# Sliding-window decode attention with a gated mixer: head outputs collected by one product a unit, one product for shared maxima, another order at the end, and 30 instead of 28 weight blocks summed in shares

## The chip, the core and the metric

The kernel runs on one core of one Trainium2 chip. A core has five engines that run side by side, each in its own program order: PE (TensorE, matrix products; its weight loads are listed as PEld), DVE (VectorE), ACT (ScalarE), POOL (GpSimd) and SP (SyncE, which here only issues transfers). They meet through semaphores. Sixteen DMA engines move data between HBM, where inputs and outputs lie, and SBUF; PE writes its sums to PSUM banks, from which DVE and ACT read. The metric is the device time in microseconds (us) of one execution; lower is better.

## The reference

One token is decoded for each of two batches. With `x` the input of width 512, everything in float32:

```python
xn = _layernorm(x)
# attention: 32 query heads on 8 key/value heads, the last W = 4096 of 32768 cached positions
q = (xn @ wq)                                      # wq 512 x 4096
scores = einsum("bhqd,bhkd->bhqk", q, k) * 128**-0.5
s = einsum("bhqk,bhkd->bhqd", softmax(scores), v)  # head width 128
s = s.reshape(2, 1, 4096) @ wo                     # wo 4096 x 512
# gated mixer: one more small feed-forward of xn
z = gelu(xn @ w_in); z1, z2 = halves(z); z2 = _layernorm(z2)
g = silu((z1 * (w_sp * z2 + b_sp)) @ w_out)
return x + s * g
```

Of the caches only the window is read: 2 batches x 8 heads x 4096 x 128 x 4 bytes, 33.5 MB of keys and as many of values. With `wq` and `wo` (8.4 MB each), `w_in` and `w_out` the page counts 89.40 MB read from HBM.

## The kernel before

**Tiles and ring.** Work is cut into 8 *units*; a unit is one batch and two key/value heads, so its keys fill one tile of 128 partitions x 8192 numbers (4 MB) and its values another. All large loads go through one ring of four such slots, in the order `win, wout, wq0, wq1, k0, k1, v0, k2, v1, ... k7, v6, v7, wo0, wo1, wo2`, all issued by SP in that order. A load can be issued only when the last reader of the tile four places before it in the ring is done; what stands behind it on SP waits with it. So `wo2`, the last 2 MB of the output weights, takes the slot of `v6`, the values of unit 6, and `wo1` that of `k7`. `wo` is cut into 32 blocks of 256 KB: `wo0` brings 16 of them in two transfers of 8, `wo1` brings 8 in one, and `wo2` brings blocks 24 to 31 in transfers of 4, 2, 1 and 1 blocks (`pieces`). A block is a tile of 128 x 512.

**One unit.** `turn` has DVE transpose a quarter of the keys in 32 x 32 squares (`kt`, four a unit). `shares` multiplies it on PE by the query heads, in four groups of 32 columns of the array (`sh`), and ACT copies the result to SBUF (`shs`). `add_shares` adds the shares of the four groups in another product (`s`). `share_max` finds the maximum of each head's scores: DVE reduces (`m`), spreads the maxima with a mask (`mg`), PE multiplies by `same_r` so that all partitions of a head see all its maxima (`mo`), DVE reduces again (`mx`) and makes the bias (`nb`). `probs` is the exponential on ACT (`p`, sums `l`), `weights` and `weigh` add the sums over the partitions of a head and invert them (`ls`, `wd`), `probs_t` transposes `p` (`pT`). `values` is the product with the values: 16 products of 512 columns, in four column groups (`acc`). `scale_out` copies `acc` to SBUF on ACT, scaled (`o`, four calls). `collect` puts the unit's eight head outputs into rows of a PSUM bank that the units of a batch share (`col`), and `gather` reduces that bank, after a batch's last unit, to `oT`, the outputs in the layout that the final product needs. PE sums float32 in two records per product, so the profile counts each product twice.

**Order.** Every helper records its instruction to be kept in program order, so each engine does its work in the order of the code, and the profile shows nearly all of it at one line, L37. The loop over units runs one unit ahead: while unit n's keys are turned and multiplied, unit n-1 (`prev`) gets its maxima, exponentials and values. After the loop stands what is left of unit 7.

**The end.** `part` sums blocks 0 to `EARLY`-1 of the final product in four column groups, block n in group n mod 4, each with all 512 output columns. When all are summed, ACT copies the bank (`parts`), and `spread_quarters` adds the four groups while it cuts the 512 columns in quarters (`so`, 4 products of 128 columns). The blocks from `EARLY` on are added straight to `so`, four products of 128 columns for each block. DVE multiplies by the gate and adds `x` (`res`), and SP and ACT write the two rows of the output.

Of the kernel before, what the change touches and what calls it, by code (L numbers as in the profile page):

```python
# [12 lines left out]
AX = mybir.AxisListType  # L13

P = 128
HQ, DH = 32, 128
G = 4
# [4 lines left out]
def ap(t, offset, dims):  # L22

    return bass.AP(tensor=t.tensor, offset=t.offset + offset, ap=[list(t.ap[0])] + [list(d) for d in dims])
# [18 lines left out]
def kernel(  # L43
# [13 lines left out]
    nc = tc.nc  # L57
    pe, dve, act, sp = (InOrder(tc, e) for e in (nc.tensor, nc.vector, nc.scalar, nc.sync))
    B, _, D = x.shape
# [9 lines left out]
    NU = B * HKV // 2  # L69
    J = 2 * W // P  # L70
    JC = 512 // 32
    NCH = J // JC
# [8 lines left out]
    def slot(name):  # L81
        return ring.tile([P, SLOT], F32, tag="slot", name=name)

    def const(name, *shape):
        return cst.tile([P, *shape], F32, tag=name, name=name)

    def bank(name, tag):
        return ps.tile([P, 512], F32, tag=tag, name=name, bufs=BANKS[tag])
# [12 lines left out]
    for a in range(2):  # L101
        t = slot(f"wq{a}")
# [29 lines left out]
    nc.gpsimd.memset(x4, 0.0)  # L132
    add_dq = const("add_dq", NCH - 1 + P)
    nc.gpsimd.memset(add_dq, 0.0)
    sel = const("sel", 35)
    nc.gpsimd.memset(sel, 0.0)
    oT = const("oT", 32, 32)
    nc.gpsimd.memset(oT, 0.0)

    rowm = const("rowm", 32)  # L140
# [32 lines left out]
    rowr = const("rowr", 8)  # L173
    dve.tensor_reduce(rowr, rowm.rearrange("p (r m) -> p r m", m=NCH), axis=AX.X, op=ALU.add)
    same_r = const("same_r", G, 8, NCH)
    dve.tensor_copy(same_r, ap(rowr, 0, [[0, G], [1, 8], [0, NCH]]))
    same_r = same_r.rearrange("p g r m -> p (g r m)")
    diag = const("diag", NCH)
    dve.tensor_reduce(diag, rowm.rearrange("p (r m) -> p m r", m=NCH), axis=AX.X, op=ALU.add)
    dve.tensor_copy(sel[:, 3:35:4], rowr)  # L180
    for a in range(2):
        dve.tensor_copy(
            ap(add_dq, NCH - 1 + 16 * a, [[32, G], [4, REP]]),
# [14 lines left out]
    for k in range(KT):  # L198
        for g in range(G):
            pe.matmul(  # L200
                pz[32 * g : 32 * g + 32, :], xnT[:, k, :], ap(win[:, k, :], g * FQ, [[FH, 2], [1, FQ]]),
                start=(k == 0), stop=(k == KT - 1),
# [43 lines left out]
    def spread_quarters(dst, shares, start=True, stop=True):  # L246
        for g in range(G):
            pe.matmul(
                dst[32 * g : 32 * g + 32, :], rowm, shares[:, g * DC : (g + 1) * DC], start=start, stop=stop,
            )  # L250
# [18 lines left out]
    for k in range(KT):  # L269
        for r in range(2):  # L270
            for g in range(G):
# [3 lines left out]
                    start=(k == 0), stop=(k == KT - 1),  # L275
# [24 lines left out]
    def turn(u, m):  # L300

        u.kt[m] = sb.tile([P, JC, DH], F32, tag="kt", name=f"kt{u.n}_{m}", bufs=3)
        dve.transpose(
            u.kt[m].rearrange("p j d -> p (j d)"), u.k[:, JC * m : JC * m + JC, :].rearrange("p j d -> p (j d)")
        )

    def shares(u, m):

        u.sh = bank(f"sh{u.n}_{m}", "sh")
        for dq in range(4):  # L310
            pe.matmul(
                u.sh[32 * dq : 32 * dq + 32, :], q_of(u, dq), u.kt[m][:, :, 32 * dq : 32 * dq + 32],
                start=True, stop=True,
            )
        u.shs[m] = sb.tile([P, 512], F32, tag="shs", name=f"shs{u.n}_{m}")
        act.activation(u.shs[m], u.sh, AF.Copy)

    def add_shares(u, m):

        if m == 0:  # L320
            u.s = bank(f"s{u.n}", "s")
        pe.matmul(u.s, add_dq[:, NCH - 1 - m : NCH - 1 - m + P], u.shs[m], start=(m == 0), stop=(m == NCH - 1))

    def share_max(u):
        m2 = sb.tile([P, 2], F32, tag="m2", name=f"m2_{u.n}")
        dve.tensor_reduce(m2, ap(u.s, 0, [[1, 2], [2, 256]]), axis=AX.X, op=ALU.max)
        mg = sb.tile([P, 2, G * NCH], F32, tag="mg", name=f"mg{u.n}")
        dve.tensor_mul(mg, ap(m2, 0, [[1, 2], [0, G * NCH]]), spot.rearrange("p a g m -> p a (g m)"))
        u.mo = bank(f"mo{u.n}", "mo")
        for a in range(2):  # L330
            pe.matmul(u.mo[:, : G * NCH], same_r, mg[:, a], start=(a == 0), stop=(a == 1))
        mx = sb.tile([P, 1], F32, tag="mx", name=f"mx{u.n}")
        dve.reduce_max(mx, u.mo[:, : G * NCH], axis=AX.X)
        u.nb = sb.tile([P, 2], F32, tag="nb", name=f"nb{u.n}")
        dve.scalar_tensor_tensor(u.nb, ap(mx, 0, [[0, 2]]), -SCALE, negm, op0=ALU.mult, op1=ALU.add)

    def probs(u):

        u.p = sb.tile([P, 512], F32, tag="p", name=f"p{u.n}")
        u.l = sb.tile([P, 2], F32, tag="l", name=f"l{u.n}")  # L340
        for a in range(2):
            act.activation(
                ap(u.p, a, [[2, 256]]), ap(u.s, a, [[2, 256]]), AF.Exp,
                bias=u.nb[:, a : a + 1], scale=SCALE, accum_out=u.l[:, a : a + 1],
            )

    def probs_t(u):
        u.pT = sb.tile([P, JC, 32], F32, tag="pT", name=f"pT{u.n}")
        dve.transpose(u.pT.rearrange("p j r -> p (j r)"), u.p)

    def weights(u):
        pe.matmul(u.mo[:, 32:34], same_r, u.l, start=True, stop=True)

    def weigh(u):
        l = sb.tile([P, 1], F32, tag="ls", name=f"ls{u.n}")
        dve.reduce_sum(l, u.mo[:, 32:34], axis=AX.X)
        dve.reciprocal(l, l)
        u.wd = sb.tile([P, NCH], F32, tag="wd", name=f"wd{u.n}")
        dve.tensor_scalar_mul(u.wd, diag, l)

    def values(u):
        u.acc = bank(f"acc{u.n}", "acc")
        for j in range(JC):
            c = j % G
            pe.matmul(
                u.acc[32 * c : 32 * c + 32, :], u.pT[:, j, :], u.v[:, j : J : JC, :],
                start=(j < G), stop=(j >= JC - G),
            )

    def scale_out(u):  # L370
        u.o = sb.tile([P, 4, DH], F32, tag="o", name=f"o{u.n}")
        for jj in range(4):
            act.activation(
                u.o[:, jj, :], u.acc[:, jj * DH : (jj + 1) * DH], AF.Copy, scale=u.wd[:, jj : jj + 1]
            )

    col = {}

    def collect(u):
        if u.w == 0:  # L380
            col[u.b] = bank(f"col{u.b}", "col")[:, : 4 * 32].rearrange("p (j d) -> p j d", j=4)
        for e in range(4):
            pe.matmul(
                col[u.b][32 * u.w : 32 * u.w + 32], sel[:, 3 - e : 35 - e], u.o[:, :, 32 * e : 32 * e + 32],
                start=(e == 0), stop=(e == 3),
            )

    def gather(u):
        if u.w == NU // B - 1:
            dve.reduce_sum(oT[:, :, 16 * u.b], col[u.b].rearrange("p j d -> p d j"), axis=AX.X)  # L390

    units = []
    for n in range(NU):
        u = Unit()
# [13 lines left out]
    j = 0  # L408
    for i, piece in enumerate(pieces):
        t = slot(f"wo{i}").rearrange("p (j d) -> p j d", d=D)  # L410
        at = 0
        for n in piece:
            sp.dma_start(t[:, at : at + n, :], wo_v[:, j : j + n, :])
            blocks += [(t, at + a) for a in range(n)]
            at, j = at + n, j + n
# [2 lines left out]
                    sp.dma_start(x4[16 * b : P : 32, :], by_group(x, b, 0, DC))  # L418

    prev = old = None  # L420
    for u in units:
        turn(u, 0)
        shares(u, 0)
        if old is not None:
            gather(old)
        if prev is not None:
            share_max(prev)
            probs(prev)
            weights(prev)
        turn(u, 1)  # L430
        shares(u, 1)
        add_shares(u, 0)
        if prev is not None:
            probs_t(prev)
            weigh(prev)
            values(prev)
        for m in range(2, NCH):
            turn(u, m)
            shares(u, m)
            add_shares(u, m - 1)  # L440
        if prev is not None:
            scale_out(prev)
        add_shares(u, NCH - 1)
        if prev is not None:
            collect(prev)
        old, prev = prev, u
    share_max(prev)
    probs(prev)
    weights(prev)
    probs_t(prev)  # L450
    weigh(prev)
    values(prev)
    scale_out(prev)
    collect(prev)
    gather(prev)


    EARLY = 28
    part = bank("part", "sh")
    for n in range(EARLY):  # L460
        t, a = blocks[n]
        g = n % G
        pe.matmul(part[32 * g : 32 * g + 32, :], oT[:, n, :], t[:, a, :], start=(n < G), stop=(n >= EARLY - G))
    parts = sb.tile([P, D], F32, tag="shs", name="parts")
    act.activation(parts, part, AF.Copy)
    so = bank("so", "mo")[:, :DC]
    spread_quarters(so, parts, stop=False)
    for n in range(EARLY, 32):
        t, a = blocks[n]
# [37 lines left out]
```

## Time and profile before

| what | us |
|---|---|
| median of 3 runs (lowest to highest) | 218.58 (218.48 to 218.61) |
| the profiled execution's own time | 218.74 |
| its span, first to last instruction | 216.9 |
| PE busy in the span | 155.2 |
| DVE busy | 105.8 |
| ACT busy | 43.9 |
| DVE idle before the key transposes | 45.9, of it 38.6 until keys landed |

The profile is of one execution. A row of a group of instructions gives the line, the engine, the operation, the tiles (out<-in), the shapes and the count, then the busy time and the mean of one in ns, then the engine's idle time just before them and what ended it. "DMA x" as a releaser is the landing of a transfer. In views by time, columns are the start and the length in us. Engines that are idle off the path to the end cost nothing, so the busy shares alone don't tell the bound.

### The profile page before, as it was taken

How to read it: one execution, taken by the hardware profiler on the slowest of the kernel's cores; microseconds unless marked ns; L12 is line 12 of the kernel's file. 1: busy time of each engine (PE TensorE's matmuls, PEld its weight loads, DVE VectorE, ACT ScalarE, POOL GpSimd, SP SyncE). 2: the span in 40 equal slices, each digit the busy share in tenths (PEclk: the TensorE clock that was granted, in tenths of full speed). 3: DMA queues.
4: the chain of work that ended last, by engine and by line, in shares of the span. 5: the costliest groups of instructions: out<-in, count | busy, mean ns of one | idle time of the engine just before them, and what ended most of it. 6: DMA issues, size and time to landing. Idle time of an engine off the chain costs nothing.

```text
span 216.9 us, 2315 instructions
## 1 busy us (share of the span) xinstructions
PE 155.2 (72%) x914; PEld 48.6 (22%) x914; DVE 105.8 (49%) x165; ACT 43.9 (20%) x109; POOL 2.5 (1%) x13
## 2 busy tenths in 40 slices
PE   0173189409959948975997698499759958979672
PEld 0121022101212222222223122222321231232221
DVE  3405402659687089247806932890595189121001
ACT  5003310002221421032114203211330421140200
POOL 4000000000000000000000000000000000000000
PEclk9997559955988995998599799859966996996999
DMA  7999999999999999999999999999999999999980
GB/s 249 428 435 465 405 461 408 447 423 435 423 429 435 420 447 411 453 411 447 424 438 429 435 426 423 435 435 432 423 441 417 453 411 435 432 411 415 425 334 3
DMA packets 3937, 89.54 MB, mean 413 GB/s; under 512 B 454, under 2 KB 470, under 8 KB 856
## 3 DMA queue, kind: packets, MB, share of 16 engines
q1 hardware_dynamic: 3912, 89.40, 96.4%
q8 instruction: 7, 0.11, 0.2%
q14 instruction: 2, 0.02, 0.0%
q10 hardware_dynamic: 16, 0.01, 0.0%
HBM read 89.40 MB, written 0.00 MB: 412 GB/s over the span
## 4 chain that ended last, share of the span: by engine, by line
DMA 66%; DVE 18%; PE 14%; issue 1%; ACT 0%; DVEq 0%; ACTq 0%
DMA k<-in_A_k_cache_dram 50%; DVE kt L37 16%; DMA wo<-in_A_wo_dram 11%; DMA win<-in_B_w_in_dram 5%; PE sh L37 5%; PE s L37 3%; PE z L37 2%; PE acc L37 2%; PE mo L37 1%; DVE pT L37 1%; PE so L37 1%; PE part L37 1%; DVE mx L37 0%; DVE ls L37 0%; DVE wd L37 0%
## 5 line engine op out<-in xcount | busy, mean ns | idle before, releaser
L37 DVE STREAM_TRANSPOSE kt<-k 128x2048 f32<-128x2048 f32 x32 | 72.7, 2295 | 45.9 <-DMA k<-in_A_k_cache_dram 38.6
L37 PE MATMUL sh<-kt,qbd 128*32 128x512 f32 x256 | 41.3, 721 | 19.1 <-DVE kt L37 19.1
L37 ACT ACTIVATE shs<-sh 128x512 f32<-128x512 f32 x32 | 19.1, 597 | 123.4 <-PE sh L37 123.4
L37 PE MATMUL s<-shs,add_dq 128*128 128x512 f32 x64 | 40.6, 741 | 0.0
L37 PE MATMUL acc<-v,pT 128*32 128x512 f32 x256 | 34.1, 680 | 0.4 <-DVE ls L37 0.4
L37 PEld LDWEIGHTS s<-shs,add_dq 128*128 128x128 f32 x64 | 11.3, 219 | 30.8 <-issue 26.4
L37 PEld LDWEIGHTS acc<-v,pT 128*32 128x32 f32 x256 | 8.3, 125 | 29.2 <-issue 18.4
L37 PEld LDWEIGHTS sh<-kt,qbd 128*32 128x32 f32 x256 | 6.3, 115 | 35.0 <-issue 19.5
L37 PE MATMUL mo<-l,same_r 128*128 128x2 f32 x16 | 3.5, 287 | 12.2 <-ACT p L37 12.2
L37 ACT ACTIVATE o<-acc,wd 128x128 f32<-128x128 f32 x32 | 9.1, 373 | 6.2 <-PE acc L37 6.2
L37 PE MATMUL col<-o,sel 128*32 128x128 f32 x64 | 8.5, 275 | 1.3 <-ACT o L37 1.3
L37 DVE TENSOR_REDUCE m<-s 128x2 f32<-128x512 f32 x8 | 5.3, 664 | 7.6 <-PE s L37 7.6
L37 PE MATMUL z<-win,xnT 128*32 128x448 f32 x32 | 5.0, 789 | 5.4 <-DMA win<-in_B_w_in_dram 5.4
L37 ACT ACTIVATE p<-s,nb 128x256 f32<-128x256 f32 x16 | 7.6, 485 | 4.3 <-DVE nb L37 4.3
L37 PEld LDWEIGHTS col<-o,sel 128*32 128x32 f32 x64 | 6.3, 109 | 7.6 <-ACT o L37 6.9
L37 PE MATMUL q_ps<-wq,xnT 128*32 128x512 f32 x64 | 7.7, 633 | 0.0
L37 PE MATMUL part<-wo,oT 128*32 128x512 f32 x56 | 6.4, 595 | 1.3 <-DMA wo<-in_A_wo_dram 0.8
L37 PE MATMUL y<-wout,hT 128*32 128x512 f32 x14 | 3.6, 1058 | 3.8 <-issue 3.8
L37 DVE STREAM_TRANSPOSE pT<-p 128x512 f32<-128x512 f32 x8 | 5.4, 674 | 1.1 <-ACT p L37 1.1
L37 PEld LDWEIGHTS mo<-l,same_r 128*128 128x128 f32 x16 | 2.8, 219 | 13.0 <-ACT p L37 13.0
L37 PEld LDWEIGHTS mo<-mg,same_r 128*128 128x128 f32 x32 | 4.2, 190 | 6.2 <-DVE mg L37 6.2
L37 ACT ACT_TABLE_LOAD x4 | 5.1, 1283 | 2.0 <-issue 1.9
(100 smaller groups left out, 54.8 us busy)
## 6 DMA issues: line engine op xcount, KB each, us to landing
k<-in_A_k_cache_dram SPq DMA_DIRECT2D x8, 4096.0 KB, 26.5
v<-in_A_v_cache_dram SPq DMA_DIRECT2D x8, 4096.0 KB, 33.5
wq<-in_A_wq_dram SPq DMA_DIRECT2D x2, 4096.0 KB, 29.2
wo<-in_A_wo_dram SPq DMA_DIRECT2D x3, 2048.0 KB, 28.2
win<-in_B_w_in_dram SPq DMA_DIRECT2D x1, 3584.0 KB
wout<-in_B_w_out_dram SPq DMA_DIRECT2D x1, 1792.0 KB, 15.3
wo<-in_A_wo_dram SPq DMA_DIRECT2D x1, 1024.0 KB, 22.9
wo<-in_A_wo_dram SPq DMA_DIRECT2D x1, 512.0 KB, 23.8
```

What stands on the lines that cost most here:

```text
L37: return self.tc.keep_in_program_order(call(*args, **kwargs))
```

## The change

Four things change.

1. `collect` becomes one product a unit: the whole `o` (128 x 512) against 32 columns of a mask, into the rows of the unit's batch in one `col` bank. `gather` then does more, once a batch: DVE reduces the bank to `heads` (32 x 128), four small products with the new mask `place` spread the heads over 128 partitions in a PSUM bank of the `acc` kind, and DVE copies the result to `oT`. `place` is cleared by POOL and filled by DVE at the start, `sel` grows from 35 to 56 columns.
2. `share_max` adds the two halves of `mg` on DVE and makes one product with `same_r` of it, where there were two.
3. In the last pass of the loop (unit 7), the values of unit 6, their scaling and their collecting are left out. They stand after the loop, the values in two halves: one ahead of unit 7's maxima, one behind its exponentials. `scale_out` and `collect` of unit 6 stand among unit 7's steps.
4. `EARLY` goes from 28 to 30. Blocks 28 and 29 (the transfer of two blocks) are now summed into `part`, ahead of the copy `parts`; only blocks 30 and 31 come behind the spread.

```diff
-        for a in range(2):
-            pe.matmul(u.mo[:, : G * NCH], same_r, mg[:, a], start=(a == 0), stop=(a == 1))
+        dve.tensor_add(mg[:, 0], mg[:, 0], mg[:, 1])
+        pe.matmul(u.mo[:, : G * NCH], same_r, mg[:, 0], start=True, stop=True)
...
-    def values(u):
-        u.acc = bank(f"acc{u.n}", "acc")
-        for j in range(JC):
+    def values(u, part=0, parts=1):
+        if part == 0:
+            u.acc = bank(f"acc{u.n}", "acc")
+        n = JC // parts
+        for j in range(n * part, n * part + n):
...
     def collect(u):
...
+        r = slice(32 * u.b, 32 * u.b + 32)
+        pe.matmul(
+            col[0][r, :], sel[:, 24 - 8 * u.w : 56 - 8 * u.w], u.o.rearrange("p j d -> p (j d)"),
+            start=(u.w == 0), stop=(u.w == NU // B - 1),
+        )
+
+    def gather(u):
+
+        if u.w < NU // B - 1:
+            return
+        r = slice(32 * u.b, 32 * u.b + 32)
+        dve.reduce_sum(heads[r, :], col[0][r, :].rearrange("p (j d) -> p d j", j=NCH), axis=AX.X)
+        t = bank(f"oT{u.b}", "acc")[:, :32]
         for e in range(4):
             pe.matmul(
-                col[u.b][32 * u.w : 32 * u.w + 32], sel[:, 3 - e : 35 - e], u.o[:, :, 32 * e : 32 * e + 32],
-                start=(e == 0), stop=(e == 3),
-            )
-
-    def gather(u):
-        if u.w == NU // B - 1:
-            dve.reduce_sum(oT[:, :, 16 * u.b], col[u.b].rearrange("p j d -> p d j"), axis=AX.X)
+                t, place[r, 3 - e : 3 - e + P], heads[r, 32 * e : 32 * e + 32], start=(e == 0), stop=(e == 3)
+            )
+        dve.tensor_copy(oT[:, :, 16 * u.b], t)
...
-            values(prev)
+            if u is not last:
+                values(prev)
...
-    share_max(prev)
-    probs(prev)
...
+    values(old, 0, 2)
+    share_max(last)
+    probs(last)
+    values(old, 1, 2)
+    weights(last)
+    probs_t(last)
+    weigh(last)
+    scale_out(old)
+    values(last)
+    collect(old)
+    scale_out(last)
+    collect(last)
+    gather(last)
+
+
+    EARLY = 30
```

On PE the end of the program, from the last key products of unit 7 on, reads before (a row is one run of like products; "32x512 x16" is sixteen products with 32 rows and 512 columns of output):

```order
L37 MATMUL acc_948<-v_305,pT_941 32x512 x16
L37 MATMUL sh_2_967<-kt_2_965,qbd 32x512 x4
L37 MATMUL s_939<-shs_1_937,add_dq 128x512
L37 MATMUL sh_3_977<-kt_3_975,qbd 32x512 x4
L37 MATMUL s_939<-shs_2_972,add_dq 128x512
L37 MATMUL s_939<-shs_3_982,add_dq 128x512
L37 MATMUL col_810<-o_985,sel 32x128 x4
L37 MATMUL mo_999<-mg_997,same_r 128x16 x2
L37 MATMUL mo_999<-l_1007,same_r 128x2
L37 MATMUL acc_1018<-v_307,pT_1011 32x512 x16
```

and after:

```order
L37 MATMUL sh_2_941<-kt_2_939,qbd 32x512 x4
L37 MATMUL s_930<-shs_1_928,add_dq 128x512
L37 MATMUL sh_3_951<-kt_3_949,qbd 32x512 x4
L37 MATMUL s_930<-shs_2_946,add_dq 128x512
L37 MATMUL s_930<-shs_3_956,add_dq 128x512
L37 MATMUL acc_960<-v_309,pT_932 32x512 x8
L37 MATMUL mo_973<-mg_971,same_r 128x16
L37 MATMUL acc_960<-v_309,pT_932 32x512 x8
L37 MATMUL mo_973<-l_981,same_r 128x2
L37 MATMUL acc_1005<-v_311,pT_993 32x512 x16
```

The values of unit 6 (the first `acc` row of each list) moved from ahead of unit 7's third key product to behind its last score product, in two halves around the product of the maxima.

The rows that follow these on PE, up to the end of the program, read before:

```order
L37 MATMUL col_810<-o_1035,sel 32x128 x4
L37 MATMUL part<-wo_309,oT 32x512 x16
L37 MATMUL part<-wo_314,oT 32x512 x8
L37 MATMUL part<-wo_316,oT 32x512 x4
L37 MATMUL so<-parts,rowm 32x128 x4
L37 MATMUL so<-wo_316,oT 32x128 x16
```

and after:

```order
L37 MATMUL col<-o_1000,sel 32x512
L37 MATMUL col<-o_1023,sel 32x512
L37 MATMUL oT_1030<-heads,place 128x32 x4
L37 MATMUL part<-wo_313,oT 32x512 x16
L37 MATMUL part<-wo_318,oT 32x512 x8
L37 MATMUL part<-wo_320,oT 32x512 x6
L37 MATMUL so<-parts,rowm 32x128 x4
L37 MATMUL so<-wo_320,oT 32x128 x8
```

Two blocks of `wo2` moved from behind the spread (`so<-parts`) to ahead of it, and `oT` is now made by way of four small products.

On DVE the steps of unit 7 from its maxima on read after (before, the rows with `mg` as only input, with `heads` and with COPY are not there, and a reduction `oT<-col` stands in place of the last two):

```order
L37 TENSOR_REDUCE m_7_969<-s_930 128x2
L37 TENSOR_TENSOR mg_971<-m_7_969,spot 128x32
L37 TENSOR_TENSOR mg_971<-mg_971 128x16
L37 TENSOR_REDUCE mx_976<-mo_973 128x1
L37 TENSOR_SCALAR nb_978<-mx_976,negm 128x2
L37 STREAM_TRANSPOSE pT_993<-p_980 128x512
L37 TENSOR_REDUCE ls_995<-mo_973 128x1
L37 RECIPROCAL ls_995<-ls_995 128x1
L37 TENSOR_SCALAR wd_998<-diag,ls_995 128x4
L37 TENSOR_REDUCE heads<-col 32x128
L37 COPY oT<-oT_1030 128x32
```

One addition per unit and one copy per batch came to DVE. On SP the transfers stand in the same order before and after.

More of the change, by code (lines that the diff above doesn't have):

```diff
@@ L134 @@
     nc.gpsimd.memset(add_dq, 0.0)
-    sel = const("sel", 35)
+    sel = const("sel", 56)
     nc.gpsimd.memset(sel, 0.0)
+    place = const("place", 3 + P)
+    nc.gpsimd.memset(place, 0.0)
+    heads = const("heads", DH)
     oT = const("oT", 32, 32)
@@ L179 @@
     dve.tensor_reduce(diag, rowm.rearrange("p (r m) -> p m r", m=NCH), axis=AX.X, op=ALU.add)
-    dve.tensor_copy(sel[:, 3:35:4], rowr)
+    dve.tensor_copy(sel[:, 24:32], rowr)
+    dve.tensor_copy(place[:, 3 : 3 + P : 4], rowm)
     for a in range(2):
@@ L379, in collect @@
     def collect(u):
-        if u.w == 0:
-            col[u.b] = bank(f"col{u.b}", "col")[:, : 4 * 32].rearrange("p (j d) -> p j d", j=4)
+        if u.n == 0:
+            col[0] = bank("col", "col")
+        r = slice(32 * u.b, 32 * u.b + 32)
[9 more added lines that the diff above has]
+        t = bank(f"oT{u.b}", "acc")[:, :32]
         for e in range(4):
             pe.matmul(
-                col[u.b][32 * u.w : 32 * u.w + 32], sel[:, 3 - e : 35 - e], u.o[:, :, 32 * e : 32 * e + 32],
-                start=(e == 0), stop=(e == 3),
-            )
-    def gather(u):
-        if u.w == NU // B - 1:
-            dve.reduce_sum(oT[:, :, 16 * u.b], col[u.b].rearrange("p j d -> p d j"), axis=AX.X)
+                t, place[r, 3 - e : 3 - e + P], heads[r, 32 * e : 32 * e + 32], start=(e == 0), stop=(e == 3)
+            )
+        dve.tensor_copy(oT[:, :, 16 * u.b], t)
     units = []
@@ L420 @@
     prev = old = None
+    last = units[-1]
     for u in units:
@@ L440 @@
             add_shares(u, m - 1)
-        if prev is not None:
+        if u is not last and prev is not None:
             scale_out(prev)
         add_shares(u, NCH - 1)
-        if prev is not None:
+        if u is not last and prev is not None:
             collect(prev)
         old, prev = prev, u
-    share_max(prev)
-    probs(prev)
[L449 to L458, printed above, removed]
+    values(old, 0, 2)
[12 more added lines that the diff above has]
+    EARLY = 30
     part = bank("part", "sh")
```

## The prediction

> **What bounds the kernel now.** I read the page's head first, then the chain that ended last, then the end of the timeline, and last the transfer queue against that timeline.
>
> ```profile
> span 216.9 us, 2315 instructions
> ...
> DMA  7999999999999999999999999999999999999980
> ...
> DMA 66%; DVE 18%; PE 14%; issue 1%; ACT 0%; DVEq 0%; ACTq 0%
> ...
> L37 DVE STREAM_TRANSPOSE kt<-k 128x2048 f32<-128x2048 f32 x32 | 72.7, 2295 | 45.9 <-DMA k<-in_A_k_cache_dram 38.6
> ```
>
> The DMA engines are at 9 tenths or more in 38 of the 40 slices. PE, at 72% of the span, is far from that, and DVE stands 38.6 us waiting for keys. The transfers set the pace; the engines have room in every unit.
>
> The chain's last pieces (start, length, what):
>
> ```profile
> 183.50 3.62 PE acc L37 x32
> ...
> 187.13 22.94 DMA wo<-in_A_wo_dram
> 210.07 0.04 issue
> 210.12 1.11 PE part L37 x8
> ...
> 211.31 0.61 ACT parts L37
> ...
> 211.96 1.34 PE so L37 x40
> ...
> 213.32 0.30 DVE res L37
> ```
>
> The 1 MB transfer with blocks 24 to 27 is issued when the values of unit 6 are done (187.13) and lands at 210.07. What comes after it is bare: four blocks, the copy, the spread and four more blocks, 213.30 at the end. Between issue and landing lie 22.94 us for one MB, so it only stands in a queue. Are the other two MB of the tail on time? Their issues by SP, and the mean times to landing:
>
> ```profile
> 187.51 0.43 SPq L37 DMA_DIRECT2D wo<-in_A_wo_dram  x1
> 197.12 0.33 SPq L37 DMA_DIRECT2D wo<-in_A_wo_dram  x1
> wo<-in_A_wo_dram SPq DMA_DIRECT2D x1, 512.0 KB, 23.8
> DMA to landing us min/median/max: 15.5/22.9/28.2
> ```
>
> Blocks 28 and 29 (512 KB) land at 187.51 + 23.8 = 211.3; block 31, issued last and with the shortest time to landing, at 197.12 + 15.5 = 212.6. In the kernel before both are there when PE reaches them: blocks 28 and 29 are needed behind the spread, after 211.96, and the 40 products from 211.96 on run without a stop (1.34 us for 40, each 0.27 and four side by side).
>
> Was PE itself late for 210.07? These rows say no:
>
> ```profile
> 203.54 0.29 DVE L37 TENSOR_REDUCE oT<-col 128x32 f32<-128x128 f32 x1 [7.24 <-PE col L37]
> 203.94 5.36 PE L37 MATMUL part<-wo,oT 128*32 128x512 f32 x48 [0.43 <-issue]
> 210.12 1.07 PE L37 MATMUL part<-wo,oT 128*32 128x512 f32 x8 [0.82 <-DMA wo<-in_A_wo_dram]
> ```
>
> `oT` is ready at 203.83, 24 blocks are done at 209.30, and PE idles 0.82 us until the landing. So an earlier `oT` is worth nothing here, unless the landings also come earlier.
>
> **Blocks 28 and 29 summed in shares: the term that counts.** Before, the copy waits for the landing of 210.07; after, for that of 211.31, 1.24 us later. From landing to the start of the copy it took 210.07 to 211.31 = 1.24 us with four blocks in four column groups. With two blocks in two groups I take the same 1.24: each block still needs its two passes one after the other. The nearest rows, one group alone and four side by side:
>
> ```profile
> 187.86 1.13 PE L37 MATMUL s<-shs,add_dq 128*128 128x512 f32 x2
> L37 PE MATMUL part<-wo,oT x56: 589/592/617, 203.9 to 210.6; 128*32 128x512 f32 x56
> ```
>
> One group took 1.13, four took 1.07. The bounds of the pair are thus 0.06 more, and, if all four records ran at once, one record's 0.59 in place of 1.07, 0.48 less; I take the four-group row, being of the same tiles. The copy then starts at 211.31 + 1.24 = 212.55, and PE takes up the spread 0.65 later (211.96 - 211.31), at 213.20. What is left is 24 records instead of 40: (1.34 - 0.27) / 39 = 0.027 a step, so 23 x 0.027 + 0.27 = 0.90. PE ends at 214.10 where it ended at 213.30: +0.80. Block 31 has landed at 212.6 by then. Everything behind it (`res`, the output) moves along. Bounds of this term: +0.32 to +0.86.
>
> **The new order of the last units: nothing.** It moves the values of unit 6 (3.62 us on PE) behind the last score product of unit 7, and with them the release of `v6`'s slot, for which `wo2`'s first transfer waits, with three more of `wo2` queued behind it on SP. The rows for when that is:
>
> ```profile
> 182.82 2.27 DVE L37 STREAM_TRANSPOSE kt<-k 128x2048 f32<-128x2048 f32 x1
> 188.92 1.07 PE L37 MATMUL sh<-kt,qbd 128*32 128x512 f32 x8
> 191.93 0.69 DVE L37 TENSOR_REDUCE m<-s 128x2 f32<-128x512 f32 x1 [6.84 <-PE s L37]
> 192.91 0.62 PE L37 MATMUL mo<-mg,same_r 128*128 128x16 f32 x4
> 195.85 5.34 PE L37 MATMUL acc<-v,pT 128*32 128x512 f32 x32 [0.36 <-DVE ls L37]
> 201.25 1.14 ACT L37 ACTIVATE o<-acc,wd 128x128 f32<-128x128 f32 x4 [6.20 <-PE acc L37]
> 202.44 1.06 PE L37 MATMUL col<-o,sel 128*32 128x128 f32 x8 [1.26 <-ACT o L37]
> ...
> 187.00:204.00 17.00, 13.36 (x84) 4.87 (x80) 2.66 (x9) 4.38 (x14) 0.00 (x0) 0.90 0.99 420
> ```
>
> The last keys are turned at 185.09. PE is then free for them at about 185.3, and the scores are complete 191.93 - 188.92 = 3.0 later, at 188.3. The values of unit 6 follow, 3.6 us plus the small product for the maxima, done at about 192.3. So `wo2` is issued 5.2 us later than now. In front of it in the queue stand 22.94 x 420 GB/s = 9.6 MB at 187.13, so 17.7 us remain at 192.3: hidden. If that cover were gone, each us of delay would be a us of the total. The two single blocks are not concerned: the last is issued at 197.12 by another wait.
>
> `oT` comes earlier: the maxima's product at about 190.2 (behind the first half of unit 6's values), then 195.85 - 192.91 = 2.9 to unit 7's values at 193.1, 3.6 of values (5.34 at the slower clock of that row), 1.2 for the scaling, about 1.1 for a product of 512 columns in two passes, 0.7 for the reduction of 512 numbers (as `m`), the four placing products and 0.2 for the copy. The trace has no such product. In eight records, they cost no less than the four `mo` records, 0.62; from above, two `mo` rows and their waits in full, some 8 x 0.46 = 3.7 by the means of weight load (190 ns) and product (268 ns) below. Near the `mo` row I take 0.9: `oT` at about 200.8, with the upper price 203.6, with the slower clock on top of it 205.3. 24 blocks took 5.36 with a stop, so 28 take at most 5.36 x 28 / 24 = 6.3; they must be done at 211.3, and `oT` may come as late as 205.0. Cost nothing, gain nothing.
>
> **One product for shared maxima, one product a unit for collecting.**
>
> ```profile
> L37 PE MATMUL mo<-mg,same_r 128*128 128x16 f32 x32 | 5.0, 268 | 0.0
> L37 PEld LDWEIGHTS mo<-mg,same_r 128*128 128x128 f32 x32 | 4.2, 190 | 6.2 <-DVE mg L37 6.2
> ...
> L37 DVE TENSOR_TENSOR mg<-m,spot 128x32 f32<-128x32 f32 x8 | 1.5, 192 | 0.3
> ...
> L134 POOL MEMSET add_dq<- 128x131 f32 x1 | 0.2, 207 | 0.0
> ```
>
> Per unit DVE gains an addition of at most 0.19 us (the row of `mg`, on twice the numbers) and PE loses two records of `mo`; collecting goes from 1.06 us to the 1.1 of a 512-column product in two passes. Once, in unit 5, DVE stands about 1.5 us longer in `gather`, waiting for PE in front of the next maxima. All of it lies under the 38.6 us of waiting for keys, or, for unit 7, under the slack just shown. Without that cover 8 x 0.19 + 1.5 = 3 us would show. POOL's new clear is of the size of `add_dq`'s, 0.2 us, and its results are first read at the end of the first unit and of the first batch.
>
> **The sum.** The transfers end where they did, the tail is 0.80 longer: 218.74 + 0.80 = 219.5 for the profiled execution, which lies 0.16 above the median; against the median, 218.58 + 0.80 = 219.4.
>
> **Rivals.** *PE at half clock in the tail.* The trace shows the clock fall after a stretch in which PE mostly idled:
>
> ```profile
> 193.50:197.00 3.50, 1.56 (x15) 0.71 (x18) 1.49 (x6) 1.02 (x4) 0.00 (x0) 0.99 1.01 431
> 197.00:200.40 3.40, 3.40 (x20) 0.87 (x16) 0.00 (x0) 0.00 (x0) 0.00 (x0) 0.51 1.00 425
> 206.94 0.16 PEld L37 LDWEIGHTS part<-wo,oT 128*32 128x32 f32 x4 [0.27 <-DMA wo<-in_A_wo_dram]
> ```
>
> 1.56 of 3.50 us busy, and the next 3.40 at a granted 0.51; the values of unit 7, which lay there, took 5.34 where those of unit 6 took 3.62. After the change PE has summed 16 blocks by about 204.5 and idles until blocks 16 to 23 land at 206.9: some 2.3 us that were not idle before. A stretch of 3.4 us with as much idle time (1.94) begins between 203.0 and 205.0, and the next one, slow, ends between 209.8 and 211.8. Where it ends by 210.6 the wait for 211.3 takes up the loss; beyond that the last blocks slip. Worst, the four blocks take some 0.9 more and the two begin late and partly slow, about +0.6: 220.0. For it speaks the row; against it, that only a beginning between 203.8 and 205.0, 1.2 of 3.4, does harm. [...]
>
> *The landings move (faster).* The sixteen engines don't end together:
>
> ```profile
> 210.10:211.30 1.20, 1.07 (x8) 0.16 (x8) 0.00 (x0) 0.00 (x0) 0.00 (x0) 1.00 0.52 198
> 211.30:212.60 1.30, 0.64 (x24) 0.64 (x28) 0.00 (x0) 0.60 (x1) 0.00 (x0) 1.00 0.06 24
> ```
>
> After 210.1 some 0.27 MB are left (1.2 x 198 + 1.3 x 24 GB/s), which all engines together would move in 0.6 us instead of 2.0. If the later issue of `wo2` evened them out, all landings would come up to 1.4 earlier, and the earlier `oT` would let PE use them: 0.80 - 1.4 = -0.6, 218.0. It decides from 1.24 us on (0.80 plus 0.44). Against it: the transfers, their sizes and their order are the same.
>
> *No change to be measured.* The two blocks' four passes overlap, +0.32, and a landing is a little earlier: 218.8.
>
> **Chances.** Forecast 0.58 (its own range 219.0 to 219.8); half clock 0.16; a slow `oT` or a dry queue, over 220.2, 0.05; no change 0.13; earlier landings 0.08. About 0.2% (0.44 us) is what a measurement of this kernel can tell. Hence faster 0.08, same 0.13, slower 0.79. The range goes from the lower bound of the term, 218.58 + 0.32 = 218.9, to a little over the half clock's 220.0: 220.2.
>
> **What the changed profile would show.** Right: `wo2`'s first issue near 192 and `oT` near 201, yet the 512 KB transfer landing at 211.3; `parts` starting near 212.5 with PE waiting for DMA just before; a bare tail from `parts` on; 24 records of `so`. Wrong: `parts` near 211.3 again (landings earlier, or passes side by side), idle slices of the DMA engines before 205, or a clock of 0.5 past 207.

## The result and the profile after

The changed kernel takes 219.28 us (median of 6 runs, 218.87 to 219.60); the kernel before, run beside it, 218.46 us (6 runs, 218.29 to 218.61). The ratio is 1.0038, 95% interval 1.0025 to 1.0051: 0.82 us slower. The execution whose profile follows took 219.14 us, with a span of 217.4 us.

The page's head and its chain, after:

```profile
span 217.4 us, 2207 instructions
...
DMA  7999999999999999999999999999999999999970
...
DMA 62%; DVE 19%; PE 16%; issue 1%; ACT 0%; DVEq 0%; SPq 0%; ACTq 0%
```

The transfers still fill the span, as before. The last pieces of the chain, after (start, length, what):

```profile
192.49 0.33 PE mo L37 x2
192.81 0.06 SPq L37
...
192.93 17.94 DMA wo<-in_A_wo_dram
210.86 0.04 issue
210.91 1.08 PE part L37 x4
...
212.07 0.60 ACT parts L37
...
212.72 0.91 PE so L37 x24
...
213.65 0.30 DVE res L37
```

The transfer on the chain is now that of blocks 28 and 29, no longer that of blocks 24 to 27. Their four records take 1.08 us, as eight took 1.11 before; from landing to `parts` 1.21 us pass, and the 24 records behind the spread take 0.91. The end of the timeline on PE and DVE:

```profile
198.96 0.68 DVE L37 TENSOR_REDUCE heads<-col 32x128 f32<-32x512 f32 x1 [5.50 <-PE col L37]
199.70 1.29 PE L37 MATMUL oT<-heads,place 32*128 32x32 f32 x8 [0.78 <-DVE heads L37]
201.03 0.21 DVE L37 COPY oT<-oT 128x32 f32<-128x32 f32 x1 [1.38 <-PE oT L37]
201.34 9.38 PE L37 MATMUL part<-wo,oT 128*32 128x512 f32 x56 [0.35 <-issue]
```

`oT` is there at 201.24, 2.6 us earlier than before, although the new collecting needs 2.28 us from the last collecting product to `oT` (198.96 to 201.24). None of these 2.6 us arrives at the end.

### The profile page after: what moved, and what is told of

Read it like the earlier page. It is cut to its first block, busy times and chain, and to the rows that moved or that the text cites. A ratio compares the mean times of both kernels' runs of the same rounds, so it can differ in the third digit from the quotient of the medians.

```text
span 217.4 us, 2207 instructions
## 1 busy us (share of the span) xinstructions
PE 156.1 (72%) x854; PEld 43.4 (20%) x854; DVE 108.6 (50%) x176; ACT 44.0 (20%) x109; POOL 2.6 (1%) x14
## 4 chain that ended last, share of the span: by engine, by line
DMA 62%; DVE 19%; PE 16%; issue 1%; ACT 0%; DVEq 0%; SPq 0%; ACTq 0%
DMA k<-in_A_k_cache_dram 49%; DVE kt L37 15%; DMA wo<-in_A_wo_dram 8%; DMA win<-in_B_w_in_dram 5%; PE sh L37 5%; PE s L37 4%; PE z L37 2%; PE acc L37 2%; PE mo L37 1%; DVE pT L37 1%; DVE m L37 1%; PE part L37 0%; PE oT L37 0%; PE so L37 0%; DVE mg L37 0%
## 5 line engine op out<-in xcount | busy, mean ns | idle before, releaser
L37 PE MATMUL acc<-v,pT 128*32 128x512 f32 x256 | 33.0, 659 | 0.2 <-DVE pT L37 0.2
L37 PEld LDWEIGHTS acc<-v,pT 128*32 128x32 f32 x256 | 7.8, 121 | 26.9 <-issue 19.3
L37 PE MATMUL part<-wo,oT 128*32 128x512 f32 x60 | 10.4, 808 | 0.6 <-issue 0.4
L37 PE MATMUL col<-o,sel 128*32 128x512 f32 x16 | 8.3, 601 | 0.4 <-ACT o L37 0.4
L37 PE MATMUL xnT_ps<-ident,xn 2*128 2x2 f32 x4 | 0.6, 253 | 6.6 <-DVE xn L37 6.6
```

What stands on the lines that cost most here:

```text
L37: return self.tc.keep_in_program_order(call(*args, **kwargs))
```

## Experiments

Each kernel was run in turns with the kernel before on the same chip; differences are between the medians of one occasion. The kernel before had medians of 218.55, 218.60, 218.68 and 218.53 us there. A ratio and its interval come from all the runs of an occasion and are not the quotient of the two medians, so the two can differ by 0.1% or so.

### The changed kernel with EARLY back at 28

```diff
-    EARLY = 30
+    EARLY = 28
```

> The changed kernel with EARLY back at 28: one product for collecting and for maxima, and the new order, stay. Theory (the 30 blocks in shares are the whole loss): as the kernel before, within 0.2 us; oT near 201, wo2's first issue near 192, parts starting 1.24 us behind the landing of blocks 24 to 27, near 211.3 or a few tenths earlier. Rival (the order or the later issue of wo2 costs it): 0.5 to 0.8 us slower than before, as the changed kernel is.

Measured: 218.74 us (12 runs, 218.02 to 219.42), 0.19 us above the kernel before; ratio 0.9999, interval 0.9977 to 1.0020. In its profile the copy starts 1.24 us behind the landing of blocks 24 to 27, as expected, but `wo2` was issued at 194.48 and `oT` came at 203.0, each some two us later than expected, in part because the clock of PE (its granted share of full speed) was at 0.50 there until 186.6 us, in the profile of the changed kernel until 183.4. With `EARLY` undone the loss is gone, as the theory has it. But the runs scatter over 1.4 us, where those of the kernel before mostly lie within half of one.

### EARLY = 30 alone

```diff
-    EARLY = 28
+    EARLY = 30
```

> The kernel before with EARLY = 30 and nothing else. Theory: 0.80 us slower than before (0.5 to 1.1), parts starting 1.24 us behind the landing of the 512 KB transfer, near 212.5, and 24 records of so behind it in 0.9 us. Rival (the order costs it): no change.

Measured: 219.29 us (12 runs), 0.73 us slower than before; ratio 1.0029, interval 1.0002 to 1.0057. Its chain:

```profile
211.38 0.04 issue
211.43 1.08 PE part L37 x4
...
212.58 0.61 ACT parts L37
...
213.24 0.91 PE so L37 x24
```

The landing at 211.38, 1.20 us to the copy, 0.91 us for the 24 records: the forecast term, in the kernel before with nothing else changed. The interval is wide because two of the twelve runs took 220.46 and 220.99 us.

### EARLY = 32 alone

The spread closes the sum, since no block comes behind it.

```diff
-    EARLY = 28
+    EARLY = 32
...
-    spread_quarters(so, parts, stop=False)
+    spread_quarters(so, parts)
```

> The kernel before with EARLY = 32: all 32 blocks in shares, the copy waits for the very last landing (212.6). Theory (the tail hangs on the landing of the last block in shares): parts starts 1.24 us behind that landing, at 213.85, the spread 0.65 later, its eight records take 0.46, so PE ends at 214.96 where it ended at 213.30: 1.65 us slower than before (1.2 to 1.9), twice what EARLY = 30 costs. Rival (the loss of EARLY = 30 comes from two blocks in two column groups, not from the landing): with four blocks in four groups again no more than 0.8 us slower.

Measured: 219.97 us (4 runs), 1.38 us slower; ratio 1.0066, interval 1.0053 to 1.0079. Four blocks in four groups cost more than two in two, so it is the landing that counts, not the number of groups. In the timeline the first row is blocks 24 to 27, the second blocks 28 to 31, stretched to 2.30 us by the landings of their three transfers; the copy starts 1.18 us behind the last of these, at 212.06:

```profile
209.60 1.06 PE L37 MATMUL part<-wo,oT 128*32 128x512 f32 x8 [0.57 <-DMA wo<-in_A_wo_dram]
210.85 2.30 PE L37 MATMUL part<-wo,oT 128*32 128x512 f32 x8 [0.18 <-DMA wo<-in_A_wo_dram]
213.24 0.60 ACT L37 ACTIVATE parts<-part 128x512 f32<-128x512 f32 x1 [11.56 <-PE part L37]
```

That landing came 0.5 us earlier in this profile than the 212.6 of the kernel before; the median, 1.38, is 0.27 under the 1.65 that was expected, and within the bounds given.

### EARLY = 24, in the kernel before and in the changed one

```diff
-    EARLY = 28
+    EARLY = 24
```

(In the changed kernel the line that goes reads `EARLY = 30`.)

> The kernel before with EARLY = 24: all eight blocks of wo2 come behind the spread. Theory (the copy must not wait for a late landing, and the last landing at 212.6 is the floor): parts starts right behind block 23, near 209.4, and PE ends about 0.45 us behind the last landing: 212.6 + 0.05 + 0.38 = 213.05 where it ended at 213.30, so 0.25 us faster than before. Rival (the 32 more records of quarters cost as much as the copy's wait saves): no gain, or up to 0.9 us slower.

> The changed kernel with EARLY = 24. Theory: as the kernel before with EARLY = 24, 0.25 us faster than before; the earlier oT changes nothing, since the end hangs on the last landing. Rival (the earlier oT is worth something once the copy is out of the way): 0.3 us or more faster than the kernel before with EARLY = 24.

> The changed kernel with EARLY = 24, on another occasion: 0.2 us faster than before, the fastest of all here, with a scatter of 0.5 us. Rival: no faster than before.

Measured: in the kernel before 218.38 us (12 runs), 0.17 faster, ratio 0.9990 (0.9963 to 1.0018). In the changed kernel 218.34 us (12 runs), 0.22 faster, ratio 0.9984 (0.9963 to 1.0004); on the second occasion 218.27 us, 0.41 faster, ratio 0.9988 (0.9976 to 1.0000). The chain of the second of these three, at its end:

```profile
197.49 14.83 DMA wo<-in_A_wo_dram
212.33 0.04 issue
212.37 0.47 PE so L37 x8
...
212.87 0.30 DVE res L37
```

Now the very last transfer is on the chain and only eight records stand behind it; less can hardly be left to do behind a landing. The gain was forecast as 0.25 us; the medians agree, but each interval reaches 1.0000 or a little beyond, so the gain is not shown. On the second occasion the scatter, 217.92 to 219.34 us, was three times the 0.5 us that was expected.

### The new order alone

The loop and the steps after it as in the change; collecting, maxima and `EARLY` as before.

```diff
-            values(prev)
+            if u is not last:
+                values(prev)
...
+    values(old, 0, 2)
+    share_max(last)
+    probs(last)
+    values(old, 1, 2)
```

> The kernel before with the new order of the last two units alone (values of unit 6 behind unit 7's scores); collecting, maxima and EARLY = 28 as before. Theory: median within 0.2 us of before. The changed kernel with EARLY = 28 scattered from 218.0 to 219.4 where the kernel before lies within 218.3 to 218.9 apart from three runs: if that comes with the new order (wo2's issue later, instructions loaded at other times), it shows here too; if with the collecting, this kernel lies as close as before.

Measured: 218.97 us (12 runs, 218.34 to 219.86), 0.36 us slower; ratio 1.0017, interval 1.0004 to 1.0031. Not within 0.2 us, and the scatter comes with the order. The profile shows how. PE in the timeline, and two stretches (start and end, length, busy time of PE, PEld, DVE, ACT and POOL with counts, granted clock, DMA share, GB/s):

```profile
202.38 1.92 PE L37 MATMUL part<-wo,oT 128*32 128x512 f32 x16 [0.61 <-DMA wo<-in_A_wo_dram]
207.28 4.48 PE L37 MATMUL part<-wo,oT 128*32 128x512 f32 x24 [2.98 <-DMA wo<-in_A_wo_dram]
```

```profile
203.80:207.20 3.40, 0.50 (x8) 0.00 (x0) 0.00 (x0) 0.00 (x0) 0.00 (x0) 1.00 0.95 395
207.70:211.10 3.40, 3.40 (x20) 0.80 (x16) 0.00 (x0) 0.00 (x0) 0.00 (x0) 0.50 0.83 325
```

`oT` was ready at 199.74, PE ran out of blocks and idled 2.98 us until 16 to 23 landed. The clock then went to 0.50 from 207.7 on, just when the last blocks arrived: blocks 16 to 27 took 4.48 us without a stop, and the copy started at 211.89, 2.16 us behind the landing of 209.73 instead of 1.24. An earlier `oT` was here a loss. The list of all runs points the same way: the six above 219 us had a mean granted clock of 0.853 to 0.859, five of the six below had 0.864 to 0.866.

### The same, with the idle time filled

```diff
+    fill = bank("fill", "acc")
     for n in range(EARLY):
+        if n == 16:
+            for f in range(10):
+                t, a = blocks[f]
+                g = f % G
+                pe.matmul(fill[32 * g : 32 * g + 32, :], oT[:, f, :], t[:, a, :], start=True, stop=True)
```

The ten products write to a bank that nobody reads.

> The new order alone, as in the run before it, plus ten products of 512 columns into an unused bank behind block 15, where PE idled 3 us (204.3 to 207.3) for the landing of blocks 16 to 23. Theory (the order's 0.37 us and its scatter of 1.5 us come from the clock, which falls after that idle stretch and is low when blocks 24 to 27 land): median within 0.2 us of the kernel before, scatter under 0.8 us, and a granted clock of 1.0 from 207 on. Rival (they come from the landings, which the later issue of wo2 moves): still 0.3 us or more slower, with the scatter.

Measured: 218.62 us (12 runs, 218.25 to 219.05), 0.06 us below the kernel before; ratio 0.9982, interval 0.9961 to 1.0004. The scatter fell from 1.52 to 0.80 us, just at the bound that was named. The fill and the same two stretches:

```profile
204.28 2.74 PE L37 MATMUL fill<-wo,oT 128*32 128x512 f32 x20
207.44 1.92 PE L37 MATMUL part<-wo,oT 128*32 128x512 f32 x16 [0.42 <-DMA wo<-in_A_wo_dram]
209.94 1.06 PE L37 MATMUL part<-wo,oT 128*32 128x512 f32 x8 [0.57 <-DMA wo<-in_A_wo_dram]
```

```profile
203.80:207.20 3.40, 3.22 (x28) 0.75 (x20) 0.00 (x0) 0.00 (x0) 0.00 (x0) 1.00 0.98 408
207.70:211.10 3.40, 2.73 (x24) 0.42 (x16) 0.00 (x0) 0.00 (x0) 0.00 (x0) 1.00 0.83 327
```

`wo2` is issued as without the fill (193.23 and 193.03), the transfers are the same, blocks 24 to 27 land at 209.89, no earlier than the 209.73 without it, PE has more work, and the loss is gone. So the order's cost lay in the clock after the idle time (0.50 from 207.7 us on without the fill, 1.00 with it), not in the landings.

### The collecting and the maxima alone

Order and `EARLY` as before, `collect`, `gather` and `share_max` as in the change.

```diff
+        pe.matmul(
+            col[0][r, :], sel[:, 24 - 8 * u.w : 56 - 8 * u.w], u.o.rearrange("p j d -> p (j d)"),
...
+        dve.reduce_sum(heads[r, :], col[0][r, :].rearrange("p (j d) -> p d j", j=NCH), axis=AX.X)
```

> The new collecting and the single product for maxima alone; order and EARLY = 28 as before. From the end of the last collecting product to oT the changed kernel takes 2.3 us (reduction, four placing products, copy) where the kernel before takes 0.35. Theory: oT 1.9 us later than in the kernel before, near 205.7, of which 0.8 is to spare, so 1.1 us slower (0.7 to 2 with the clock). Rival (the prediction's: these two parts cost nothing): within 0.2 us of before.

Measured: 220.59 us (6 runs, 219.63 to 222.69), 1.91 us slower; ratio 1.0096, interval 1.0060 to 1.0132. The profile is of the 219.63 us execution:

```profile
203.62 0.70 DVE heads L37
...
204.35 1.07 PE oT L37 x8
...
205.78 6.25 PE part L37 x56
...
212.11 0.61 ACT parts L37
```

`oT` comes at 205.68, 1.85 us later than in the kernel before, and now PE works through all 28 blocks without a stop and ends behind the landings. The chain has gone over to PE. The forecast 1.1 us holds for the profiled execution (1.0 above the median of before); the median lost 0.8 us more, within the 2 us allowed for a slower clock. That the clock did it is not shown: no slower execution was profiled, and the slowest run, 222.69 us, had the highest mean clock of the six, 0.861.

### One product with the values made twice

In the kernel before, and in the changed kernel with `EARLY` = 28:

```diff
     values(last)
+    values(last)
```

> The kernel before with unit 7's product with the values made twice, the second result used: 32 records and 3.64 us (5.3 at the slower clock) more on PE ahead of oT, nothing else. Theory (before, oT has 0.8 us to spare): oT near 207.5, so 2.8 us slower than before, up to 4.5 with the slower clock. Rival (the end hangs on the landings alone): no change.

> The changed kernel with EARLY = 28 and the same product made twice. Theory (the new order has oT at 201.2, with 3.5 us to spare): oT near 204.9, end within 0.5 us of the kernel before. Rival (the time gained by the new order is not there in most runs, for example by the clock): 1.5 us or more slower than before.

Measured: the kernel before 221.32 us (4 runs), 2.72 slower, ratio 1.0120 (1.0101 to 1.0139), as expected. The changed kernel with `EARLY` = 28: 220.46 us (4 runs), 1.87 slower, ratio 1.0091 (1.0071 to 1.0111), where at most 0.5 was expected. Its chain and one stretch:

```profile
203.18 1.07 PE oT L37 x8
...
204.61 7.82 PE part L37 x56
...
212.51 0.61 ACT parts L37
```

```profile
204.40:207.80 3.40, 3.19 (x16) 0.91 (x20) 0.10 (x1) 0.00 (x0) 0.00 (x0) 0.50 0.96 401
```

`oT` came at 204.50, as forecast, but from 204.4 to 207.8 the clock was at 0.50 and the 28 blocks took 7.82 us, not 6.3. The rival came true, with the cause that it gave as its example: the time to spare that I had counted holds at full clock only. It is still more than in the kernel before, which fell back 0.85 us further under the same load.

### What the runs point to

The order of the change with the collecting of before, the fill, and `EARLY` = 24:

> The new order with the collecting of before, ten filling products, and EARLY = 24: what the runs so far point to. Theory: the end hangs on the last landing alone (PE ends 0.5 us behind it), so 0.2 to 0.4 us faster than the kernel before, with a scatter under 0.6 us and no run above 219.5, since PE has time to spare and its clock is held. Rival: no faster than before.

Measured: 218.37 us (12 runs, 218.01 to 218.52), 0.16 us faster; ratio 0.9984, interval 0.9966 to 1.0001. All twelve runs lie below the median of before. The 0.16 us are a little under the 0.2 to 0.4 that were expected. By the medians it is about as fast as the changed kernel with `EARLY` = 24, and it scatters over 0.51 us where that one scattered over 0.54 and 1.42; that it beats the kernel before is likely, and just not certain by the interval.

## Why the prediction held

**The bound and the term of 30 blocks: right, measured.** 0.80 us were forecast, 0.82 measured, 0.73 with that edit alone, and nothing left with it undone (0.19, interval over zero). The parts of the sum: 1.24 us from landing to copy (measured 1.21 and 1.20), 0.90 for 24 records (0.91 and 0.91). The pair in two groups takes what four blocks in four take (1.08 and 1.11), as chosen between the two bounds. That the median agrees to 0.02 us is partly luck: the intervals reach from 0.55 to 1.11 us here and from 0.04 to 1.25 us with that edit alone, and the landings move by more than that from one profile to the next.

**The landing.** In the profile of the changed kernel the 512 KB transfer landed at 210.86, 0.45 earlier than the 211.3 of the sum, so this execution lost only 0.40 against the profiled one of before. With `EARLY` = 30 alone it landed at 211.38. So `parts` began at 212.07, between the 212.5 of the sum and the 211.3 that was named as a sign of being wrong. The landing of blocks 24 to 27 lay between 209.6 and 210.3 over the profiles here. What sets it in one execution is open. One difference can be seen in the transfer view between 204 and 210 us: in the kernel before a load of instructions passes there, in the changed kernel none.

```profile
q8 instruction: 1, 0.02, 1.1%
```

It doesn't sort the landings of the other profiles, though: the earliest of blocks 24 to 27, 209.55 with `EARLY` = 32, has such a load in this stretch, and the latest, 210.33 in the changed kernel with `EARLY` = 28, has none.

**"The new order: cost nothing, gain nothing" and "collecting: nothing" were right for the two together, and hold for neither alone.** I had put the two into one sum, with `oT` at 200.8 (measured 201.24) and `wo2` issued at 192.3 (192.55). Alone, the order costs 0.36 us and the collecting 1.91. Of the collecting I had written that it lies under the waiting for keys, or under the slack of unit 7; without the new order there is no such slack, and a later `oT` counts from about 0.8 us on, as the doubled product shows (in its profile `oT` came 3.44 us later and the copy 2.39; the median lost 2.72). So the order pays for the collecting. (Two slips in my reading of the lines change nothing: 37 slices of the DMA row are at 9 tenths, not 38, and the 24 blocks in 5.36 us held no stop, since 28 took 6.25 without one.)

**The limit of 205 for `oT` was too generous.** It was reckoned at full clock; with the clock at 0.50 from 204.4 to 207.8 us, in the changed kernel with the values made twice, the same blocks took 7.82 us in place of 6.3.

**The rival of the half clock.** What it supposes was seen in the new order alone, in one profile without and one with the fill: PE busy 0.50 of 3.40 us and then a clock of 0.50, against 3.22 of 3.40 and a clock that stayed at 1.00. The 1.2 of 3.4 us counted against it took every beginning of the slow stretch as equally likely; that was my estimate, and no run shows it. In the profile of the changed kernel the clock was at 0.50 earlier, and until 0.2 us past the 207 that was named as a sign of being wrong:

```profile
197.00:200.40 3.40, 2.21 (x11) 0.84 (x9) 0.68 (x1) 0.83 (x4) 0.00 (x0) 1.00 1.02 434
200.40:203.80 3.40, 3.05 (x16) 1.13 (x19) 0.21 (x1) 0.00 (x0) 0.00 (x0) 0.50 0.99 420
203.80:207.20 3.40, 3.40 (x20) 0.90 (x16) 0.00 (x0) 0.00 (x0) 0.00 (x0) 0.50 0.97 406
207.20:210.60 3.40, 3.35 (x32) 0.70 (x24) 0.00 (x0) 0.00 (x0) 0.00 (x0) 0.99 0.90 356
```

There it cost nothing: `oT` was early, and the slow blocks 0 to 15 were done at 207.5, about when 16 to 23 landed. They filled the very time from 204.5 to 206.9 in which the rival had PE idle. But they also used up the time to spare: from then on PE had next to no idle time (3.35 of 3.40 us busy) until it waited 0.18 us for blocks 28 and 29. Whether the clock had a part in the slower of the changed kernel's runs (up to 219.60) no profile tells.

**The rival of earlier landings** fails: with `EARLY` = 28 the kernels that issue `wo2` late are no faster than the kernel before beyond their intervals (0.9999 in the changed kernel, 1.0017 with the order alone, 0.9982 with the fill, where the interval reaches 1.0004). The very last landing, which ends the kernels with `EARLY` = 24, came at 212.33, 212.12 and 212.57 in the three profiles with the late issue and at 212.41 without it.

## What to carry to other kernels

Here transfers filled the span (9 tenths or more in 37 of 40 slices), and while PE kept up with them the time was the last landing on the chain plus what stood behind it. In such a kernel a step that closes a sum (a copy, a spread over partitions) should wait for the last landing that still leaves it time, and the late pieces should be added behind it, even at more instructions. Waiting for a later landing cost 0.7 to 1.4 us here; going down to `EARLY` = 24 gained 0.2 to 0.4 us by the medians, not clear of the noise. An edit that costs nothing beside another edit may cost 2 us alone: undo the parts one by one before calling one free. And finishing early on PE is not always free: here PE idled 2.98 us just before the end, and the clock was at 0.50 when the last data landed.

## What was not expected of the hardware

**A clock that falls after partly idle time.** Before the low stretches PE had been busy 0.50 of 3.40 us (the order alone) and, in the kernel before, 1.56 of 3.50; with 3.22 of 3.40 it stayed at 1.00, and also after this stretch of the kernel before, with 1.84 of 3.40:

```profile
200.40:203.80 3.40, 1.84 (x16) 0.79 (x8) 0.26 (x1) 1.14 (x4) 0.00 (x0) 1.00 1.04 439
203.80:207.20 3.40, 3.26 (x32) 1.28 (x36) 0.04 (x1) 0.00 (x0) 0.00 (x0) 1.00 0.95 401
```

The busy time alone doesn't decide, so no bound can be read from these rows. In the changed kernel 2.21 of 3.40 us were followed by half clock, as shown above. And in the kernel before with `EARLY` = 24, whose program is the same up to the final product, the stretch in which the kernel before had its 1.56 of 3.50 was followed by full clock:

```profile
193.50:197.00 3.50, 1.54 (x12) 0.98 (x14) 1.54 (x7) 1.02 (x4) 0.00 (x0) 1.00 1.00 426
197.00:200.40 3.40, 3.24 (x32) 0.78 (x24) 0.06 (x1) 0.09 (x1) 0.00 (x0) 1.00 1.01 429
```

The values of unit 7 took 3.64 us there, 5.34 in the profile of the kernel before. The slow stretch moves from one execution to the next: in the four profiles that share the changed kernel's program up to the final product it begins at 200.4, 202.3, 202.8 and 203.7 us. So the 0.8 us that `oT` had to spare, too, are those of one execution.

In the profiles of the kernel before and of the changed one, each low stretch up to the end of the program was at 0.50 and lasted 3.4, 6.8, 10.2 or, once, 13.7 us; the last one before ran from 196.96 to 200.36 us, the last one after from 200.42 to 207.24.

**Some runs 2 us longer.** Of 98 runs of the kernel before, 7 took 220.0 to 220.7 us; of 78 runs with the new order and nothing doubled, none did (219.86 at most). The slack of `oT`, 0.8 us in the one and more in the other, would explain it together with the clock. The list of runs fits: these seven had a mean granted clock of 0.824 to 0.848, where half of the runs whose clock is listed had 0.858 or more, and the kernel before with `EARLY` = 24 and 30 had three more such runs in 24, at 0.824 to 0.839. But no such execution was profiled, so the cause is open.
